# Attention and a squared-ReLU MLP on one core: loading the first batch's third query group ahead of its values

## The chip, the core and the metric

One Trainium2 chip, one core. The metric is the device time of one execution in microseconds. An execution's span, from the first to the last instruction of its trace, is some 2 us shorter. All times compared here are of runs that count as fast. In the views of the profile PE is TensorE's matmuls and PEld its weight loads, ACT is ScalarE, DVE VectorE, POOL GpSimd, and L315 is line 315 of the kernel.

## The reference

```python
def attention(q, k, v):            # q (8, 16, 384, 64), k and v (8, 4, 384, 64), float32
    k, v = repeat(k, 4, axis=1), repeat(v, 4, axis=1)
    scores = q @ k.T / sqrt(64)
    return softmax(scores) @ v

def reference(q, k, v, moe_w_in, moe_w_out):
    x = attention(q, k, v).transpose(0, 2, 1, 3).reshape(3072, 1024)
    h = maximum(x @ moe_w_in, 0)   # (1024, 2048)
    return (h * h) @ moe_w_out     # (2048, 1024)
```

## The kernel before

The kernel records its instructions before it emits them. For each it keeps a planned start and end from costs written in the code, and a loop at the end picks TensorE's next piece of work by these planned times. A change of the load order can therefore change two things: what the queue does on the chip, and the order in which TensorE's instructions are written.

```python
def when(self, reads=(), writes=(), eng="tensor"):      # planned time at which operands are there
    t = 0.0
    for d in self.deps_of(reads, writes):
        o = self.ops[d]
        if o["eng"] == eng and o["dma"] is None:
            continue
        t = max(t, o["end"])
    return t
# ... cut
def load_v(b):                                          # the values, float32 to bf16, GpSimd's queue
    st = b % NST
    R.add("gpsimd", lambda g: g.dma_start(v_st[st]..., v[b]...),
        writes=[("v_st", st)], dma=f"v{st}", cost=1.1, issue=0.8)

def load_q(b, h0, h1, spread=0.0):                      # query heads h0 to h1
    st = b % NST
    i = R.add("gpsimd", lambda g: g.dma_start(q_st[st][:, h0:h1, :], q[b, h0:h1]...),
        writes=[...], dma=f"q{st}_{h0}", cost=0.265 * (h1 - h0), issue=0.8)
    R.ops[i]["end"] += spread                           # for the planner alone
# ... cut: the start of GpSimd's program
load_q(0, 4, 8)
# ... cut: the identity matrix
load_v(0)
load_q(0, 8, 12, 0.6)
load_q(0, 12, 16, 0.6)
dup_k(0, 1, 2)
load_w_in(0)
dup_k(0, 2, 3)
load_k(1)
dup_k(0, 3, 4)
aug_v(0, "gpsimd")                                      # copies the values beside a column of ones
load_q(1, 0, 8)
load_q(1, 8, 16)
load_w_in(1)
load_v(1)
dup_k(1)
for i in range(2, 6):
    load_w_in(i)
# ... cut: the loop's choice of TensorE's next piece
ready = [x for x in cand if x[0] <= now + (0.0 if split else 0.05)]
what = min(ready, key=lambda x: x[1]) if ready else min(cand)
idle = max(0, int((what[0] - now) / 0.11)) if now < 9 else 0
if idle:
    warm_up(idle, 0.11 * idle)                          # filler matmuls while nothing is ready
```

Query group g (four heads) is transposed on TensorE (L315), scored against three key tiles (L341), exponentiated on ScalarE (L351) and multiplied with the values (L367). L425 and L462 are the first MLP product, L524 the second, L588 the fillers.

The softmax here doesn't subtract the row's maximum and nothing guards it: scores larger than these inputs give would overflow.

## Time and profile before

| | before |
|---|---|
| time, median of 3 first runs | 420.13 us (419.4 to 420.21) |
| span of the profiled execution | 1110.1 us |
| TensorE's share of the chain that ended last | 100% |

The profiled execution is not one of the timed kind: its span is 2.6 times their 420 us. Its page has no row for TensorE's granted clock, so the 1.000 that the views print for it measures nothing.

### The profile page before, as it was taken

What the parts mean: (1) busy time and instruction counts of PE and PEld (TensorE: products, weight loads), DVE (VectorE), ACT (ScalarE), POOL (GpSimd) and SP (SyncE); (2) the same over time, 40 slices, a digit from 0 to 9 for tenths busy, and PEclk for the clock granted to TensorE, in tenths of its full rate; (3) what the DMA queues carried; (4) which work ended last, traced back from release to release, by engine and by line L of the source; (5) the groups of instructions that cost most, each with busy time, mean ns of one, the idle gap of its engine ahead of it and who ended that gap; (6) DMA issues with size and microseconds to landing.
All of it is one profiled execution on the core that took longest, in us unless ns stands there. A gap on an engine that the chain in (4) does not pass through costs nothing.

```text
span 1110.1 us, 9624 instructions
## 1 busy us (share of the span) xinstructions
PE 1107.0 (100%) x4330; PEld 446.8 (40%) x4330; DVE 203.8 (18%) x434; ACT 169.6 (15%) x181; POOL 48.0 (4%) x63
## 2 busy tenths in 40 slices
PE   9999999999999999999999999999999999999999
PEld 5544523454233532345323363243632336234323
DVE  3312201131011310114001141012300123001100
ACT  5233000330023100230003300032000320001100
POOL 7100101000100010000100000000000000000000
DMA  9950626102600070000700013000110001000000
GB/s 186 203 72 1 99 53 90 15 1 49 106 16 1 9 125 29 10 1 15 119 28 10 1 22 69 29 10 0 24 34 29 1 1 29 29 28 1 0 28 29
DMA packets 96921, 44.40 MB, mean 40 GB/s; under 512 B 77296, under 2 KB 90864, under 8 KB 96880
## 3 DMA queue, kind: packets, MB, share of 16 engines
q0 software_dynamic: 36544, 17.44, 12.2%
q1 hardware_dynamic: 59664, 25.86, 9.6%
q8 instruction: 34, 0.56, 0.2%
q10 hardware_dynamic: 672, 0.49, 0.1%
q14 instruction: 7, 0.06, 0.0%
HBM read 35.65 MB, written 12.58 MB: 43 GB/s over the span
## 4 chain that ended last, share of the span: by engine, by line
PE 100%; DVE 0%; issue 0%
PE ps L524 41%; PE ps L462 35%; PE ps L367 8%; PE ps L341 8%; PE ps L425 6%; PE ps L588 1%; PE ps L315 0%; PE ps L298 0%; PE ps L400 0%; DVE y_sb L533 0%
## 5 line engine op out<-in xcount | busy, mean ns | idle before, releaser
L524 PE MATMUL ps<-w_out_sb,h2T 128*128 128x512 bf16 (+2 forms) x784 | 460.1, 823 | 0.0
L462 PE MATMUL ps<-xT,w_in_sb 64*128 64x384 bf16 x1728 | 415.1, 681 | 0.0
L524 PEld LDWEIGHTS ps<-w_out_sb,h2T 128*128 128x128 bf16 x784 | 135.6, 175 | 309.0 <-issue 308.8
L462 PEld LDWEIGHTS ps<-xT,w_in_sb 64*128 64x128 bf16 x1728 | 153.7, 170 | 232.1 <-issue 221.8
L351 ACT ACTIVATE expT<-ps 128x1024 bf16<-128x1024 f32 (+1 forms) x146 | 146.8, 1012 | 583.7 <-PE ps L341 583.6
L475 DVE TENSOR_SCALAR hr<-ps 128x384 f32<-128x384 f32 x108 | 55.2, 553 | 371.5 <-PE ps L462 371.5
L341 PE MATMUL ps<-qT,kT 64*128 64x256 bf16 (+2 forms) x384 | 114.0, 651 | 0.0
L533 DVE COPY y_sb<-ps 128x512 f32<-128x512 f32 (+2 forms) x49 | 33.4, 681 | 406.5 <-PE ps L524 406.5
L367 PEld LDWEIGHTS ps<-v_aug,expT 128*128 128x128 bf16 x1152 | 87.1, 141 | 16.5 <-issue 12.9
L367 PE MATMUL ps<-v_aug,expT 128*128 128x65 bf16 x1152 | 90.8, 281 | 0.0
L425 PE MATMUL ps<-xT,w_in_sb 128*128 128x384 bf16 x160 | 73.1, 684 | 0.0
L341 PEld LDWEIGHTS ps<-qT,kT 64*128 64x128 bf16 x384 | 29.6, 150 | 54.5 <-issue 33.7
L482 DVE TENSOR_TENSOR h2T<-hr 128x384 bf16<-128x384 f32 x102 | 50.0, 551 | 0.0
L425 PEld LDWEIGHTS ps<-xT,w_in_sb 128*128 128x128 bf16 x160 | 27.4, 173 | 41.1 <-issue 41.0
L382 DVE TENSOR_TENSOR o_sb<-ps,rinv 128x384 bf16<-128x384 f32 x64 | 35.7, 557 | 2.2
L435 ACT ACTIVATE h2T<-hr 128x384 bf16<-128x384 f32 x20 | 10.5, 523 | 137.2 <-DVE hr L433 137.2
L479 ACT ACTIVATE h2T<-hr 128x384 bf16<-128x384 f32 x6 | 3.1, 523 | 158.9 <-DVE hr L475 158.9
L275 POOL COPY v_aug<-v_st 128x768 bf16<-128x768 bf16 x8 | 6.6, 830 | 460.0 <-PE ps L367 415.2
L376 DVE RECIPROCAL rinv<-ps 128x6 f32<-128x6 f32 x64 | 12.4, 194 | 51.1 <-PE ps L367 51.1
L433 DVE TENSOR_SCALAR hr<-ps 128x384 f32<-128x384 f32 x20 | 11.2, 558 | 54.5 <-PE ps L425 54.5
L241 POOL DMA_DIRECT2D q_st<-in_q_dram x17 | 14.8, 881 | 0.9 <-POOLq L829 0.8
L209 POOL DMA_DIRECT2D k_st<-in_k_dram x7 | 5.3, 755 | 156.2 <-DMA qT<-q_st 156.2
(29 smaller groups left out, 79.3 us busy)
## 6 DMA issues: line engine op xcount, KB each, us to landing
out_dram<-y_sb SPq DMA_DIRECT2D x47, 256.0 KB, 2.0
q_st<-in_q_dram POOLq DMA_DIRECT2D x14, 384.0 KB, 7.5
w_in_sb<-in_moe_w_in_dram POOLq DMA_DIRECT2D x8, 512.0 KB, 14.3
w_out_sb<-in_moe_w_out_dram POOLq DMA_DIRECT2D x4, 1024.0 KB, 27.6
v_st<-in_v_dram POOLq DMA_DIRECT2D x8, 192.0 KB, 8.4
k_st<-in_k_dram POOLq DMA_DIRECT2D x7, 192.0 KB, 3.8
q_st<-in_q_dram POOLq DMA_DIRECT2D x3, 192.0 KB, 5.4
xT<-o_sb SPq DMA_TRANSPOSE x28, 2.7
```

Source lines behind the costliest of these rows:

```text
L241: i = R.add("gpsimd", lambda g: g.dma_start(q_st[st][:, h0:h1, :], q[b, h0:h1].rearrange("h (p j) d -> p h (j d)", j=NJ)), writes=[("q_st" ...
L341: mm = pe.matmul(ps[:, base + x, m * wide:(m + 1) * wide], kT[b % 2][64 * x:64 * x + 64, u, :], q_cols(b, u // NJ, x, c0, c0 + wide))
L351: R.add("scalar", lambda e: e.activation(dst, src, AF.Exp, scale=0.125), reads=keys, writes=[("expT", (b * NU + u) % NEX, t) for u, _, _ i ...
L367: m = pe.matmul(po[:, f - 6 * s2, 0:D + 1], w, v_aug[b % 2][:, g * NJ + j, 0:D + 1], start=(j == 0), stop=(j == NJ - 1))
L376: R.add("vector", lambda e: e.reciprocal(rinv[r].ap().unsqueeze(2), po[:, :, D:D + 1]), reads=[("bank", i)], writes=[("rinv", r)], cost=0.22)
L382: R.add("vector", lambda e: e.tensor_tensor(dst, srcv, rbv, ALU.mult), reads=[("bank", i), ("rinv", r)], writes=[("o_sb", o, s2)], cost=0.48)
L425: m = pe.matmul(bank(i)[:, 0:S], w_in_sb[:, kc, c * 128:(c + 1) * 128], xT[b % NXT][:, kc, :], start=(kc == 0), stop=(kc == NKC - 1))
L462: m = pe.matmul(bank(4 + xs[x])[:, 0:S], w_in_sb[r, kc, c * 128:(c + 1) * 128], xT[b % NXT][r, kc, :], start=(phase < 2 and kc == 0), stop ...
L475: R.add("vector", lambda e, r=r, i=i: e.tensor_scalar_max(hr[r][:, :], bank(4 + i)[:, 0:S], 0.0), reads=[("bank", 4 + i)], writes=[("hr", ...
L482: hr_read[r] = (R.add("vector", lambda e, c=c, r=r: e.tensor_tensor(h2T[:, c, :], hr[r][:, :], hr[r][:, :], ALU.mult), reads=[("hr", r)], ...
L524: m = pe.matmul(bank(i)[:, 0:n], h2T[:, c, i3 * 128:(i3 + 1) * 128], w_out_sb[:, c, c0:c1], start=(c == 0), stop=(c == NFC - 1))
L533: R.add("vector", lambda e: e.tensor_copy(ysl, bank(i)[:, 0:n]), reads=[("bank", i)], writes=[("y", yb)], cost=0.08 + n / 960)
```

## The change

The third query group is to be there earlier; the values, copied later anyway, move behind it. The same bytes go through the same queue. The group's planning allowance of 0.6 us goes too.

```diff
-    load_v(0)
-    load_q(0, 8, 12, 0.6)
+    load_q(0, 8, 12)
+    load_v(0)
     load_q(0, 12, 16, 0.6)
```

## The prediction

> **What bounds the kernel now.** I read the page first (shares, then the chain that ended last), then the matmuls by shape, then TensorE's and GpSimd's timelines over the first 16 us, then the landings of the two loads.
>
> ```profile
> PE 1107.0 (100%) x4330; PEld 446.8 (40%) x4330; DVE 203.8 (18%) x434; ACT 169.6 (15%) x181; POOL 48.0 (4%) x63
> ...
> PE 100%; DVE 0%; issue 0%
> ```
>
> The chain is TensorE from end to end. But the profiled execution spans 1110.1 us and the timed ones 420.13 us, so the profile caught a slow TensorE. The chain of waits shows the rate, and that a matmul on 64 rows shares the array with its partner:
>
> ```profile
> 105.11 3.59 PE ps L462 x16
> ...
> 122.08 54.81 PE ps L524 x92
> ```
>
> 54.81/92 is 596 ns for 512 columns, 0.86 columns a nanosecond. L462 (64 rows, 384 columns) takes 3.59/16 = 224 ns, half of the 447 ns that 384 columns need at that rate: pairs run side by side.
>
> ```profile
> L524 PE MATMUL ps<-w_out_sb,h2T 128*128 128x512 bf16 x752 | 450.5, 835 | 0.0
> L462 PE MATMUL ps<-xT,w_in_sb 64*128 64x384 bf16 x1728 | 415.1, 681 | 0.0
> L367 PE MATMUL ps<-v_aug,expT 128*128 128x65 bf16 x1152 | 90.8, 281 | 0.0
> L425 PE MATMUL ps<-xT,w_in_sb 128*128 128x384 bf16 x160 | 73.1, 684 | 0.0
> L341 PE MATMUL ps<-qT,kT 64*128 64x512 bf16 x184 | 71.3, 790 | 0.0
> L341 PE MATMUL ps<-qT,kT 64*128 64x256 bf16 x184 | 38.4, 520 | 0.0
> ```
>
> Count times columns, halved for 64 rows: 385,024 + 331,776 + 74,880 + 61,440 + 47,104 + 23,552 = 923,776. The other forms of the view add 26,880 (the last output tile's split 8,192, first-unit scores 3,072, transposes and warm-ups 15,616): 950,656 columns. That is 856 a microsecond in the profile and 950,656/420.13 = 2,263 in the timed runs. So in the timed runs TensorE is the bound too, but waits that a slow TensorE hides may show there in the first microseconds; I have to reason about these from the durations of the other engines and the loads.
>
> ```profile
> 11.07 0.69 PE L341 MATMUL ps<-qT,kT 64*128 64x512 bf16 x2
> 11.69 0.31 PE L588 MATMUL ps<-const-bfloat16-1.0 128*128 128x128 bf16 x2
> 11.93 0.69 PE L341 MATMUL ps<-qT,kT 64*128 64x512 bf16 x2
> 12.55 0.93 PE L315 MATMUL ps<-ident,q_st 128*128 128x128 bf16 x6
> 13.19 0.73 PE L298 MATMUL ps<-ident,k_dup 128*128 128x128 bf16 x3
> 13.85 0.69 PE L341 MATMUL ps<-qT,kT 64*128 64x256 bf16 x4
> 14.47 0.93 PE L315 MATMUL ps<-ident,q_st 128*128 128x128 bf16 x6
> 15.33 0.69 PE L341 MATMUL ps<-qT,kT 64*128 64x512 bf16 x2
> 15.95 1.39 PE L367 MATMUL ps<-v_aug,expT 128*128 128x65 bf16 x18
> ```
>
> Here are the two consumers: the transpose of the third query group (12.55) and the first product with the values (15.95). Between two score bursts stand two filler matmuls (L588). GpSimd and the landings (last number: us from issue to landing):
>
> ```profile
> 3.00 0.76 POOL L234 DMA_DIRECT2D v_st<-in_v_dram  x1
> 3.76 1.50 POOL L241 DMA_DIRECT2D q_st<-in_q_dram  x2
> ...
> 8.31 0.83 POOL L275 COPY v_aug<-v_st 128x768 bf16<-128x768 bf16 x1
> 9.08 1.77 POOL L241 DMA_DIRECT2D q_st<-in_q_dram  x2
> ...
> 13.60 1.47 POOL L270 COPY k_dup<-k_st 128x1536 bf16<-128x1536 bf16 x1 [1.12 <-DMA k_st<-in_k_dram]
> ```
>
> ```profile
> v_st<-in_v_dram POOLq DMA_DIRECT2D x1, 192.0 KB, 4.8
> q_st<-in_q_dram POOLq DMA_DIRECT2D x1, 192.0 KB, 5.1
> ```
>
> Values land at 3.00 + 4.8 = 7.8 us, the third group at 3.76 + 5.1 = 8.9. Neither consumer waits for its load: the transpose starts 3.6 us after its landing, and the copy of the values (8.31) starts 0.5 us after its own.
>
> [...]
>
> **The change part by part.** It removes nothing from the device: two loads of 192 KB each (in bf16), with the same runs, swap places in one queue. It also drops 0.6 us of allowance in the kernel's planner, which issues nothing but decides the order of TensorE's instructions.
>
> (1) The loads. The group lands at about 7.8 instead of 8.9 (1.1 earlier), the values at about 8.9 instead of 7.8. Everything behind them starts after the same bytes: 0.
>
> (2) The copy of the values is next on GpSimd at 8.31. It will wait until about 8.9 and end at 8.9 + 0.83 = 9.7 instead of 9.1: 0.6 later. The loads of batch 1's queries are issued 0.6 later, 9.7 instead of 9.08. The queue is then still busy with the first weight block (5.76 + 6.8 = 12.6 by its landing) and batch 1's keys (7.10 + 6.4 = 13.5), so it does not run dry. GpSimd's next wait, 1.12 us until the keys of batch 1 land, shrinks to about 0.5 and absorbs the delay: 0 from 13.6 on.
>
> (3) The first product with the values needs the exponentials of three key tiles. ScalarE starts them at 7.16; the four short ones take about 0.8 each and one long one 1.02 (their durations in the trace): not before 7.16 + 3.1 + 1.0 = 11.3, with TensorE at any clock. The copy ends at 9.7, 1.6 us ahead: 0.
>
> (4) The third group's scores are used from unit 6. Ahead of them ScalarE has 4 short and 6 long exponentials: 3.1 + 6 x 1.02 = 9.2 us, to about 16.4 us. Loading it 1.1 us earlier saves nothing there. Its transpose comes behind the first long score burst, which needs a score bank that the third exponential frees, at 7.16 + 3 x 0.78 = 9.5: after 8.9, so no wait is removed even at a full clock.
>
> (5) The planner. I followed its rule by hand with the costs in the code (used for order only, no time is taken from them). The group counts as landed at 7.32 instead of 9.02, so at the step where the plan puts two fillers while it waits for a bank, the transpose becomes eligible and goes there: ahead of the second long score burst, with the fillers dropped (38 to 36 of L588). Later the transpose of the fourth group comes one score burst earlier, and the first half of the first value product too. By the fourth product or so ScalarE's pace sets the same score times and the plan is the old one again. On the chip: one transpose group of 6 x 128 columns, about 0.4 us at the timed rate, stands before a burst that ScalarE, with 1.02 us an exponential, has not yet made room for. TensorE waits for ScalarE there anyway: 0, or 0.1 to 0.3 either way.
>
> Sum: 0, with some tenths of uncertainty. [...]
>
> **The rivals.** (a) The values become the wait: the copy ends 0.6 us later. If the values land yet later, TensorE stalls in order at the first product and the time grows by up to 1 us, 421. Against: 1.6 us of room, unless landings shift by over that. (b) The earlier query group was really waited for at the full clock: for it, only 0.6 us separate 9.5 from 8.9. The gain would be at most about 1 us, 419; against it, ScalarE has a backlog until 16.4. (c) The GpSimd delay leaves a hole in the load queue and each weight block lands 0.6 us later; if TensorE is then waiting for weights, 420.7. Against: the landings at 12.6 and 13.5. (d) The reordered plan never rejoins the old one and later batches get other orders: anything from -3 to +3 us. Against: batches are gated by ScalarE and by whole stages, where small shifts vanish.
>
> **Range and chances.** Center 420.0: before, less a tenth for the dropped fillers and a smoother order. The runs of before spread over 0.8 us; the rivals (a) to (c) move it by 1, (d) rarely more. So 418.8 to 421.4 for 8 in 10. Two per cent is 8.4 us[...]: 0.01 faster, 0.98 the same, 0.01 slower.
>
> **What would show it.** Right: third group landing near 7.8 and values near 8.9; the copy on GpSimd starting near 8.9 with a wait on the load of some 0.6 us; 36 fillers; the transpose ahead of the second long burst; from about 20 us on the same order. Wrong: a TensorE wait for the value copy or the transposed group, a weight block landing later, or an order that differs in batch 1 and beyond. If the profile after falls in another clock state, spans are not comparable, only order and landings are.

## The result and the profile after

| | before | after |
|---|---|---|
| median of 5 runs | 420.13 us | 419.67 us |
| lowest to highest | 419.4 to 420.67 | 419.36 to 420.03 |
| ratio | | 0.9991, 95% interval 0.9977 to 1.0006 |

A ratio is the mean time of one kernel's fast runs over the mean of the other's in the same rounds, so it is not quite the ratio of the medians. The interval holds 1: no change of time is seen.

The page of the kernel after (shares, then the chain that ended last), this time of an execution at the full clock with a span of 417.5 us:

```profile
PE 414.0 (99%) x4328; PEld 236.2 (57%) x4328; DVE 199.1 (48%) x434; ACT 159.0 (38%) x181; POOL 48.0 (11%) x63
...
PE 98%; ACT 1%; DVE 0%; issue 0%
```

TensorE is still the chain, with two matmuls fewer (4328 for 4330): the two fillers. One line of that chain in order of time (start, duration, piece) gives the rate:

```profile
53.68 19.86 PE ps L524 x92
```

19.86/92 is 215.9 ns for 512 columns, against 596 in the profile before. Now TensorE's timeline of the kernel after (start, duration, instruction, count, idle time before it):

```profile
8.20 0.39 PE L341 MATMUL ps<-qT,kT 64*128 64x512 bf16 x2
8.52 0.51 PE L315 MATMUL ps<-ident,q_st 128*128 128x128 bf16 x6
8.96 0.39 PE L341 MATMUL ps<-qT,kT 64*128 64x512 bf16 x2
...
10.14 0.51 PE L315 MATMUL ps<-ident,q_st 128*128 128x128 bf16 x6
10.49 0.44 PE L367 MATMUL ps<-v_aug,expT 128*128 128x65 bf16 x9
10.86 0.39 PE L341 MATMUL ps<-qT,kT 64*128 64x512 bf16 x2
```

The transpose has taken the place of the fillers between the two long score bursts, and the first value product is split around a burst. A comparison of the two programs finds TensorE's instructions different in this short stretch alone, up to the second half of that product. GpSimd's timeline and the two landings (us from issue to landing at the end):

```profile
3.00 0.76 POOL L241 DMA_DIRECT2D q_st<-in_q_dram  x1
3.75 0.75 POOL L234 DMA_DIRECT2D v_st<-in_v_dram  x1
...
8.82 0.83 POOL L275 COPY v_aug<-v_st 128x768 bf16<-128x768 bf16 x1 [0.53 <-DMA v_st<-in_v_dram]
...
13.57 1.47 POOL L270 COPY k_dup<-k_st 128x1536 bf16<-128x1536 bf16 x1 [0.58 <-DMA k_st<-in_k_dram]
```

```profile
q_st<-in_q_dram POOLq DMA_DIRECT2D x1, 192.0 KB, 4.7
v_st<-in_v_dram POOLq DMA_DIRECT2D x1, 192.0 KB, 5.0
```

The group lands at 3.00 + 4.7 = 7.7 us, the values at 3.75 + 5.0 = 8.75. Their copy waits 0.53 us and ends at 9.65, ahead of the product at 10.49. GpSimd's wait at 13.57 has shrunk from 1.12 to 0.58 us: it swallowed the delay.

### The profile page after: what moved, and what is told of

Read it like the earlier page. It is cut to its first block, busy times and chain, and to the rows that moved or that the text cites. A ratio compares the mean times of both kernels' runs of the same rounds, so it can differ in the third digit from the quotient of the medians.

```text
span 417.5 us, 9620 instructions
## 1 busy us (share of the span) xinstructions
PE 414.0 (99%) x4328; PEld 236.2 (57%) x4328; DVE 199.1 (48%) x434; ACT 159.0 (38%) x181; POOL 48.0 (11%) x63
## 4 chain that ended last, share of the span: by engine, by line
PE 98%; ACT 1%; DVE 0%; issue 0%
PE ps L524 40%; PE ps L462 34%; PE ps L367 8%; PE ps L341 8%; PE ps L425 6%; ACT expT L351 1%; PE ps L588 1%; PE ps L298 0%; PE ps L315 0%; PE ps L400 0%; DVE y_sb L533 0%
## 5 line engine op out<-in xcount | busy, mean ns | idle before, releaser
L524 PE MATMUL ps<-w_out_sb,h2T 128*128 128x512 bf16 (+2 forms) x784 | 168.2, 375 | 0.0
L462 PE MATMUL ps<-xT,w_in_sb 64*128 64x384 bf16 x1728 | 160.0, 323 | 0.0
L524 PEld LDWEIGHTS ps<-w_out_sb,h2T 128*128 128x128 bf16 x784 | 75.2, 98 | 86.6
L462 PEld LDWEIGHTS ps<-xT,w_in_sb 64*128 64x128 bf16 x1728 | 83.3, 94 | 57.3 <-DVE hr L475 2.1
L341 PE MATMUL ps<-qT,kT 64*128 64x256 bf16 (+2 forms) x384 | 54.3, 326 | 0.4 <-ACT expT L351 0.4
L367 PEld LDWEIGHTS ps<-v_aug,expT 128*128 128x128 bf16 x1152 | 37.0, 97 | 5.5 <-ACT h2T L479 1.3
L367 PE MATMUL ps<-v_aug,expT 128*128 128x65 bf16 x1152 | 39.2, 193 | 0.0
L425 PE MATMUL ps<-xT,w_in_sb 128*128 128x384 bf16 x160 | 27.3, 326 | 0.0
L341 PEld LDWEIGHTS ps<-qT,kT 64*128 64x128 bf16 x384 | 17.8, 94 | 15.6 <-issue 2.4
L425 PEld LDWEIGHTS ps<-xT,w_in_sb 128*128 128x128 bf16 x160 | 15.4, 98 | 9.8 <-issue 0.2
L433 DVE TENSOR_SCALAR hr<-ps 128x384 f32<-128x384 f32 x20 | 11.1, 557 | 12.6 <-PE ps L425 12.5
```

Source lines behind the costliest of these rows:

```text
L341: mm = pe.matmul(ps[:, base + x, m * wide:(m + 1) * wide], kT[b % 2][64 * x:64 * x + 64, u, :], q_cols(b, u // NJ, x, c0, c0 + wide))
L367: m = pe.matmul(po[:, f - 6 * s2, 0:D + 1], w, v_aug[b % 2][:, g * NJ + j, 0:D + 1], start=(j == 0), stop=(j == NJ - 1))
L425: m = pe.matmul(bank(i)[:, 0:S], w_in_sb[:, kc, c * 128:(c + 1) * 128], xT[b % NXT][:, kc, :], start=(kc == 0), stop=(kc == NKC - 1))
L462: m = pe.matmul(bank(4 + xs[x])[:, 0:S], w_in_sb[r, kc, c * 128:(c + 1) * 128], xT[b % NXT][r, kc, :], start=(phase < 2 and kc == 0), stop ...
L524: m = pe.matmul(bank(i)[:, 0:n], h2T[:, c, i3 * 128:(i3 + 1) * 128], w_out_sb[:, c, c0:c1], start=(c == 0), stop=(c == NFC - 1))
```

## The experiments

In this part the theories have capital letters (the prediction's own rivals have small ones). Theory A: both loads have slack, and ScalarE's exponentials set the pace of the first batch. Rivals: the third group was really waited for (B); a later value copy eats the gain (C); the copy's wait on GpSimd holds up later loads (D). In most experiments the plan is made first and then one entry of a queue is moved, so that all other engines keep their order; the program comparison confirmed this for each. The helper:

```diff
+    def behind(a, b):   # a is issued right behind b; dependencies are renumbered
+        at = lambda n: next(i for i, o in enumerate(R.ops) if n in (o["dma"], o.get("tag")))
+        order = list(range(len(R.ops)))
+        order.remove(at(a))
+        order.insert(order.index(at(b)) + 1, at(a))
+        new = {o: n for n, o in enumerate(order)}
+        R.ops = [R.ops[o] for o in order]
+        for o in R.ops:
+            o["need"] = {new[d] for d in o["need"]}
```

All runs had five rounds and gave right results. All ratios are against the kernel before on the same chip. Kernels are compared only within the same rounds.

### The kernel before against itself

No edit.

> The kernel before, unchanged, against itself: the noise of a ratio, and a profile of it at the full TensorE clock, which the earlier profile did not give. Every theory: ratio 1.000 within 0.002, about 420 us. Theory A (both loads have slack, ScalarE's exponentials pace the first batch): the 20 exponentials of the first batch run without a gap over about 16.9 us and end near 22.7 us, as after the change, and neither the third group's transpose nor the first value product waits for its load. Rival B (the third group was really waited for before): TensorE waits for the group's landing near 8.9 us and the exponentials end some 0.3 to 1 us later than after the change. Rival C (a gain from the group is eaten by a later value copy): both of these waits are seen, one in each kernel.

Measured: 419.47 us, ratio 0.9996 (0.9984 to 1.0008). TensorE's timeline at the full clock:

```profile
8.50 0.39 PE L341 MATMUL ps<-qT,kT 64*128 64x512 bf16 x2
8.88 0.51 PE L315 MATMUL ps<-ident,q_st 128*128 128x128 bf16 x6
...
10.80 0.72 PE L367 MATMUL ps<-v_aug,expT 128*128 128x65 bf16 x18
```

Its waits (engine, line, what it waited for: total us, times, longest):

```profile
PEld ps L341 <- ACT expT L351: 1.0, 4, 0.3
PEld ps L315 <- DMA q_st<-in_q_dram: 0.6, 2, 0.3
```

The scores wait for ScalarE. The weight loads of the transposes waited for the second and the third query group, 0.3 us each: the third landed at 8.86 (3.76 + 5.1) and its transpose ran at 8.88. The changed kernel's first profile shows no such wait. Most of the 0.3 us is not the load's doing: a later profile with the same first loads and the same order of TensorE (the kernel before with the weights moved, below) has 0.2 us of idle at this weight load with no load named, and the matmuls show no idle of 0.15 us or more here in either. Theory A's words that nothing waits were too strong, and rival B is right that the group came just in time. What that was worth is read from the exponentials of the first batch, first of this kernel, then of the kernel after (start, duration from the first to the last of a run without a gap, count):

```profile
5.44 16.81 ACT L351 ACTIVATE expT<-ps 128x768 bf16<-128x768 f32 x20 [0.47 <-PE ps L341]
```

```profile
5.78 16.88 ACT L351 ACTIVATE expT<-ps 128x768 bf16<-128x768 f32 x20 [0.57 <-PE ps L341]
```

All 20 run without a gap in both (the view shows gaps from 0.15 us on): 16.81 and 16.88 us. The wait stood where TensorE was ahead of ScalarE. The starts differ by 0.34 us, before either moved load is used; the two profiles of the next kernel, one program, started at 5.47 and 5.75, so this is scatter. Of theory A, the part on ScalarE's pace holds.

### The loads swapped, the old order of TensorE

```diff
# kernel before
+    behind("v0", "q0_8")
     R.emit()
```

> The two loads swapped on the queue, every other engine's order that of the kernel before (fillers included). Theory A: ratio 1.000 (419.7 to 420.4 us), exponentials end at the same time as in the control within 0.1 us; the value copy starts 0.5 us later (8.8) and waits for the landing; the first value product does not wait. Rival B: 0.3 to 1 us faster, the exponentials ending that much earlier. Rival C: the first value product waits for the copy, up to 0.5 us slower.

Measured: 420.07 us (419.33 to 421.72, six runs), ratio 1.0011 (0.9994 to 1.0028). The median is as theory A has it. The profiled run was its slowest (421.72) and showed something that no theory had:

```profile
11.42 0.80 PE L315 MATMUL ps<-ident,q_st 128*128 128x128 bf16 x6 [1.65 <-DMA q_st<-in_q_dram]
```

The fourth group, not the third, landed 6.8 us after its issue at 4.49, instead of 5.3 in the kernel after, and TensorE stood for 1.65 us; its granted clock was then 0.50 from about 11.2 to 14.6 us (mean 0.57 from 11 to 15 us, 1.00 on both sides). The values came late too (6.5 us instead of 5.0). I ran this kernel once more to see whether the order causes it.

> The loads swapped under the old order once more: its profiled run had values and fourth group landing 1.5 us late, a 1.65 us wait for the fourth group, and 421.72 us, and one of its runs of before had 421.0. Theory F (a load hiccup that any of these kernels may meet): most runs at 419.3 to 420.2 again, and a profile whose fourth group lands near 9.7 with no wait of 1 us. Rival G (this order of the loads makes the late landing): the profile shows it again, with the value copy starting past 9.5, and a median of 420.5 or more.

Measured: 419.57 us (419.45 to 420.47), ratio 1.0007 (0.9995 to 1.0019); the fourth group landed 5.1 us after its issue and nothing waited for it. So this order does not bring the late landing each time (theory F); a run of before reached 421.0 as well. That the order makes it likelier is not excluded: of the six profiles with this order of the three loads one more (that of the late weight block, below) has the fourth group 6.6 us after its issue, of the four with the old order none. The profiled run again was the slowest (420.47), for another late landing:

```profile
31.28 0.83 PE L462 MATMUL ps<-xT,w_in_sb 64*128 64x384 bf16 x8 [0.65 <-DMA w_in_sb<-in_moe_w_in_dram]
```

TensorE waited 0.65 us for the fourth weight block, issued at 15.82 and landed 15.3 us later, at 31.1; in the kernel after it landed at 15.85 + 14.3 = 30.15. This led to the last group of runs.

### The new order of TensorE, the loads not swapped

```diff
# kernel after
+    behind("q0_8", "v0")
     R.emit()
```

> TensorE's order after the change, but the loads in the order of before. The third group's transpose then stands where it started at 8.52 us after the change, and the group lands at about 8.86 us. Theory A: TensorE waits there some 0.3 us for the load, which delays the second long score burst to about 9.3 us; ScalarE is busy with the first long exponential until about 9.6, so at most 0.1 us of gap among the exponentials; time within 0.2 us of the kernel after (419.6 to 420.3). Rival B: the wait shifts all that follows by 0.3 us or more.

Measured: 419.84 us (419.76 to 420.73), ratio 1.0009 (0.9996 to 1.0022). The wait is there:

```profile
8.86 0.49 PE L315 MATMUL ps<-ident,q_st 128*128 128x128 bf16 x6 [0.44 <-DMA q_st<-in_q_dram]
```

The exponentials took 16.96 us with no gap that the view shows, 0.08 us more than in the kernel after. A wait of 0.44 us for the third group is hidden. Neither the loads alone nor the order alone moves the time beyond noise, so the zero is not two large effects that cancel: the upper ends of the two intervals are 1.2 and 0.9 us, and effects of tenths are not excluded.

### The values much later

```diff
# kernel after
+    behind("v0", "wi0")
     R.emit()
```

> TensorE's order after the change, the values' load moved behind the first weight block, so that they land near 12.6 us instead of 8.8 and their copy ends near 13.4 instead of 9.65. Theory A: beyond its slack (the first value product ran at 10.49 us after the change, so 0.8 us) lateness is paid in full less what ScalarE has in store: TensorE stalls some 2.9 us, ScalarE runs dry for about 2 to 2.5 us, time 421.7 to 422.7 us (ratio 1.005 to 1.007). Rival (the start has room that no lateness of this size reaches, as TensorE has the rest of the kernel to make it up): 420, ratio below 1.002. Rival D (the copy's wait on GpSimd holds up the queries of batch 1 and the weights behind it): more than 3 us, with TensorE waits for weights after 25 us.

Measured: 425.69 us (424.4 to 426.83, four runs), ratio 1.0152 (1.0134 to 1.0171). The mechanism was as expected, the size was not:

```profile
13.71 0.66 PE L367 MATMUL ps<-v_aug,expT 128*128 128x65 bf16 x9 [3.11 <-POOL v_aug L275]
```

The stall is 3.11 us. The median rose by 6.1 us (425.69 - 419.62), the profiled run, the fastest of the four, by 4.8 (424.4 - 419.62). The value product that takes 0.44 us in the kernel after takes 0.66 here. The table by stretches (stretch; busy us of PE, PEld, DVE, ACT, POOL; TensorE's granted clock; DMA share; GB/s) shows a lower clock:

```profile
10.70:11.90 1.20, 0.00 (x0) 0.00 (x0) 0.50 (x1) 0.85 (x1) 0.00 (x0) 1.00 1.54 187
12.10:13.60 1.50, 0.00 (x0) 0.00 (x0) 0.00 (x0) 0.00 (x0) 0.86 (x2) 0.50 0.95 112
14.00:18.00 4.00, 4.00 (x45) 2.31 (x42) 1.51 (x4) 2.30 (x3) 4.00 (x5) 0.50 0.90 100
```

TensorE was idle from 10.60 us on; the granted clock fell to 0.50 at about 12.0, before work came back, and was at 1.00 again from about 18.8 (mean 0.90 from 18 to 22 us). TensorE so worked from 13.7 to 18.8 at half clock, by estimate a loss of 2.6 us (half of these 5.1). Stall and loss make 5.7 us, somewhat more than the 4.8 of this run. The other three runs have the same mean clock of 0.992 and took up to 2.4 us more, which this does not explain. The trace shows both states and the return; the clock fell 1.4 us into the wait (see the last section). No TensorE wait for weights followed, so rival D gets no support from this profile.

### The same with fillers in the idle stretch

```diff
# kernel with the values much later
-            b, c = av_q.pop(0)
+            b, c = av_q.pop(0); (b, c) == (0, 0) and warm_up(50, 0.0)
```

> The run with the values behind the first weight block, plus 50 filler matmuls of 128 columns (some 2.8 us at the full clock) put right ahead of the first value product, where TensorE stood idle for 3.1 us. That run cost 6.2 us in the medians although the stall was 3.1. Theory E (the idle stretch halves TensorE's granted clock for several microseconds, and this is the rest of the cost): with the fillers the clock column stays at 1.00 through 10 to 22 us, the first product starts at the same 13.6 us, the second gap among the exponentials (0.62 us) is gone, and the time is 422.5 to 423.5 us. Rival D (the rest is the later issue of the queries and weights behind the copy on GpSimd): no change, 425 to 426.

Measured: 424.57 us (422.4 to 425.88, six runs), ratio 1.0115 (1.0089 to 1.0141). The median lies above theory E's 422.5 to 423.5. The runs fall in two kinds: two with a mean granted clock of 1.000 over the execution took 422.4 us; the other four, at 0.996 (three, 424.65 to 425.88) or 1.000 (one, 424.49), took 2 to 3.5 us more. Without fillers all four runs had 0.992. The profiled run is of the slower kind: batch 0's keys landed 5.3 us after issue instead of 4.0, so TensorE idled earlier (0.89 and 0.70 us) and the clock was down, at 0.50 from about 9.3 to 12.7 us (mean 0.93 from 5 to 10 us, 0.66 from 10 to 14), before the fillers came at 12.96. (All 50 took 3.10 us; the 2.8 of the expectation is an estimate, which the 2,263 columns a microsecond of the timed runs give.) Where the start went well, the cost is 422.4 - 419.44 = 3.0 us, the bare stall of the run without fillers. That speaks for the clock as the rest of the cost; it does not prove it, since one run at 1.000 was slow and its profile is not known.

### The third group much later

```diff
# kernel after
+    behind("q0_8", "wi0")
     R.emit()
```

> TensorE's order after the change, the third group's load moved behind the first weight block: it lands near 12.6 us instead of 7.7, its transpose stood at 8.52. Theory A with E: TensorE stalls some 4 us from 8.5, ScalarE runs dry from about 9.5 (it has one long exponential in store), the clock falls after the idle stretch; 424 to 427 us. Rival (the group's lateness is hidden, as its scores are only needed from the seventh key tile on): 420.

Measured: 427.18 us (425.77 to 427.92), ratio 1.0177 (1.016 to 1.0194).

```profile
14.65 0.80 PE L315 MATMUL ps<-ident,q_st 128*128 128x128 bf16 x6 [6.03 <-DMA q_st<-in_q_dram]
```

The group landed at 14.5 us, later than the 12.6 that I expected, and the stall was 6.03 us. The rival fails, that lateness is hidden as the scores are needed late: in the trace TensorE takes its instructions in order (nothing ran on it from 8.62 to 14.65 us, and the burst behind the transpose came at 15.38), and the transpose stands ahead of a burst that ScalarE needs from about 9.7 us on, where its gap of 6.31 us begins. The slack of both loads is therefore under a microsecond (8.52 - 7.7 = 0.8 us for the group), not the whole distance to where ScalarE needs them.

### Values last of the three, planner free

```diff
# kernel before
-    load_v(0)
-    load_q(0, 8, 12, 0.6)
-    load_q(0, 12, 16, 0.6)
+    load_q(0, 8, 12)
+    load_q(0, 12, 16)
+    load_v(0)
```

> The change carried one step further, planner free: both query groups ahead of the values, which land last of the three, near 9.8 us, with their copy ending near 10.6. The planner puts the fourth group's transpose one burst earlier and the first value product where it stood at 10.5. Theory A: TensorE waits at most 0.2 us for the copy, exponentials without a gap, 419.4 to 420.2 us. Rival C (the values are already at their edge, so that each further delay is paid): the wait at the first product grows to 0.5 us or more and the time to 420.5 or more.

Measured: 420.13 us (419.88 to 421.63, six runs), ratio 1.0022 (1.0009 to 1.0035): inside theory A's range, but slower than before. The copy ended at 9.64 + 0.83 = 10.47 us and the first value product ran at 10.61, with 0.37 us of TensorE idle before it. The profile puts that idle to VectorE's copy of the fourth group's transpose, which ended at 9.96 + 0.56 = 10.52, so close to the value copy that the two cannot be told apart. The exponentials still had no gap (16.92 us). The profile also has a 0.32 us wait for the fourth weight block, which landed at 30.64. The later copy alone does not explain that: GpSimd was free at 13.03 + 0.78 = 13.81, but the keys of batch 1, ahead of the block in its program, landed at 13.9 instead of 13.5, and their copy started at 13.96 instead of 13.57. They landed at 13.8 in the second profile of the kernel after as well, so this is within the scatter of landings. Still, no wait of GpSimd was left to swallow a copy later than this.

### The fourth weight block: a second edge

The first product on TensorE that needs the fourth block is the third group of eight in L462. In the control, then in the kernel after:

```profile
28.67 2.29 PE L462 MATMUL ps<-xT,w_in_sb 64*128 64x384 bf16 x24
```

```profile
29.07 2.11 PE L462 MATMUL ps<-xT,w_in_sb 64*128 64x384 bf16 x24
```

The same 24 matmuls took 0.18 us longer in the control. There the block landed at about 30.0 us and was needed at 28.67 + 1.30; in the kernel after it was needed at 30.37 and had landed at 30.15. (The view names no load for the 0.18 us; that it is a wait for the block is inferred from these times.) The control's lead of 0.41 us at the end of the exponentials (22.25 against 22.66) shrank to 0.1 at the end (spans 417.4 and 417.5). Theory H: this block takes back tenths. Two runs load it earlier, one later:

```diff
# kernel after (and, in the second run, kernel before)
-    aug_v(1, "gpsimd")
+    aug_v(1, "gpsimd"); R.ops[-1]["tag"] = "copy_v1"
+    behind("v1", "wi3")
+    behind("copy_v1", "wo01")
     R.emit()
# third run: kernel after
+    behind("wi3", "wi4")
     R.emit()
```

> The changed kernel with batch 1's values loaded behind the fourth weight block instead of ahead of the third, and their copy behind the first two output-weight blocks; every other engine's order is unchanged. Theory H (the end of the first batch has a second floor: the fourth weight block lands at 30.15 us in the changed kernel and at about 30.0 in the control, and TensorE needs it at 30.37 and 29.97, so what ScalarE's chain gains or loses by tenths is taken back there): the block lands about 1 us earlier, near 29.2; the time falls by 0 to 0.3 us only, 419.1 to 419.7, since in the changed kernel the block did not wait. Rival I (no second floor, or one of a microsecond's depth): unchanged at 419.7, or below 418.8.

> The same move of batch 1's values in the kernel before. Theory H: the control's wait of 0.16 us at the fourth block disappears, 419.0 to 419.6 us, and the two kernels with the move are equal within 0.3 us, as the change itself is worth nothing. If the change were worth something that the weights had hidden, the changed kernel with the move would be faster than this one by 0.3 us or more.

> The changed kernel with the fourth and fifth weight blocks swapped on the queue: the fourth lands some 2 to 2.6 us later, near 32.4 us, and is needed at 30.37. Theory H: TensorE waits about 2 us there, 421.4 to 422.4 us (more if the idle stretch lowers the granted clock). Rival I (room of a microsecond or more): under 421.

Measured: 419.63 us, ratio 1.0001 (0.9986 to 1.0016), with the change; 419.29 us, 0.9999 (0.9982 to 1.0015), without it. The block landed at 29.2 us in the first, and the 24 matmuls took 2.11 us in both: the wait is gone, and nothing is gained that can be told from noise. The medians differ by 0.34 us in favour of the old order, a little over the 0.3 that I had set, but the means by 0.02% with intervals of 0.15%. Their profiled spans, 417.7 and 417.3, differ by about as much as the ends of their exponentials, 22.68 and 22.41: with the block out of the way, that lead stays. Later is another matter: 424.9 us (423.22 to 425.45), ratio 1.0119 (1.0098 to 1.0139), more than the 421.4 to 422.4 expected.

```profile
33.99 0.83 PE L462 MATMUL ps<-xT,w_in_sb 64*128 64x384 bf16 x8 [2.57 <-DMA w_in_sb<-in_moe_w_in_dram]
```

This profiled run was the fastest of the five and also had its start delayed, with 1.5 us of waits for query loads; the other four were slower, three of them with a mean clock of 0.996 for its 1.000, and I have no trace of them. The edge is shown, its exact price is not.

### The changed kernel once more

> The changed kernel unchanged, against before once more and beside the next three on one chip. Theory A: ratio 1.000 within 0.0015 (419.4 to 419.9 us). If the 0.9991 of the first comparison was a gain, it comes again with an interval that excludes 1.

Measured: 419.79 us (419.23 to 420.41, six runs), ratio 1.0006 (0.9989 to 1.0023). The first ratio was 0.9991. Two comparisons on either side of 1, both with 1 inside: the change is worth nothing that these runs can tell. Its profile meets the edge of the fourth block too, which landed at 30.3:

```profile
28.92 2.35 PE L462 MATMUL ps<-xT,w_in_sb 64*128 64x384 bf16 x24
```

So the wait at that block is not a thing that the change removes: the kernel after had none in one profile and 0.24 us in the other. No version here beats either kernel.

## Why the prediction was right

The time (420.0 predicted, 419.67 measured) and its mechanism held (ScalarE sets the pace, GpSimd's next wait swallows the later copy); two steps had wrong sizes, and one detail of the order was wrong.

- **Loads (1).** Predicted landings 7.8 and 8.9 us; measured 7.7 and 8.75.
- **Copy (2).** Predicted start 8.9 with a wait of 0.6, GpSimd's next wait down to 0.5; measured 8.82 with 0.53, and 0.58.
- **First value product (3): mis-sized.** "not before ... 11.3, with TensorE at any clock" was wrong. It started from ScalarE's first exponential at 7.16 us, which itself was late because of the slow TensorE (2.19 us of waiting for the scores, 0.47 in the control); at the full clock that is 5.4 to 5.8. The product ran at 10.49 and the room was 10.49 - 9.65 = 0.84 us, not 1.6. It was still enough, but this the prediction had not worked out: in this step its zero has some luck in it.
- **Transpose (4): failed in part.** "so no wait is removed even at a full clock" took over the same 7.16. TensorE reached the transpose as the group landed, not 0.6 us after it, and the weight load stood for 0.3 us, 0.2 of which are there without a late load. The main ground, ScalarE's backlog, held, but "to about 16.4" is too long: 1.02 us is how long an exponential takes, not how far they stand apart. The profile of before has two of them in 1.94 us, and the 8 short and 12 long ones took 16.81 us in the control, where 0.78 and 1.02 us each would give 18.5. Rival (b) was right that there was no room and wrong about its worth: the exponentials have no gap with the wait or without it.
- **Planner (5): right but for one piece.** Worked out by hand and found so: 36 fillers, the transpose ahead of the second long burst, the split value product. The fourth group's transpose did not come one score burst earlier: it stands behind the same burst in both (10.04 in the control, 10.14 after). The order is the old one again from the second half of the first product on, sooner than "the fourth product or so". Rival (d) fell.
- **Rivals (a) and (c).** Values landing 3.9 us later made (a) real; 0.9 us later left 0.37 us of idle, which the profile puts to another copy. For (c), the weights do stand at an edge, within about 0.2 us, in both kernels, but in this change the copy's wait was swallowed before the blocks were issued.

## What to carry to other kernels

A load that an engine really waits for can still be worth nothing (0.44 us of TensorE wait here, at a ratio of 1.0009): look whether the engine that sets the pace in that stretch, here ScalarE with 20 exponentials back to back, gets a gap. Swapping the two equal loads within one queue moved slack from one consumer to the other (the group landed at 7.7 instead of 8.86 us, the values at 8.75 instead of 7.8), so check both, and what stands behind them in program order. Start times from a profile that ran at another speed must not be used as fixed points, even those of engines whose own durations are unaffected (ScalarE's long exponential took 1024 and 1032 ns, but the first exponential started at 7.16 us in the slow profile and at 5.44 in the control).

## What the traces show of the clock and of the landings

- The first profile of before ran at 0.86 columns a nanosecond (596 ns at N = 512, and 856 columns a microsecond over the whole span); the kernel after took 215.9 ns at the same N, with a mean granted clock of 1.000. The page of before has no row for the granted clock; what slowed it is open.
- The granted clock fell to 0.50 after idle stretches of different lengths: 1.4 us into the idle stretch with the values much later (idle from 10.60, half clock from about 12.0), 1.4 us into the 1.65 us stall of the swapped loads, and after two idle stretches of 0.89 and 0.70 us in the run with fillers. With the third group much later it fell only some 4.6 us into the stall (mean 0.90 from 10 to 14 us), and the 2.57 us stall at the late weight block left it at 1.00. Half clock lasted some 3.4 us in two of the four traces and some 6.8 us in the other two. The length of a stall alone does not decide; what does was not tested.
- Landings in the loaded queue scatter: one 192 KB load (bf16) (the fourth query group) landed 5.1, 5.3 and 6.8 us after its issue in three profiles, in the same place of the queue, and the last of these stalled TensorE for 1.65 us.
